# A spectral mixer and a long convolution, two layers each: the first loads, TensorE's first matmuls and five constant loads are put in another order

## The chip, the cores and the metric

One core of a Trainium2 chip runs the whole kernel. The metric is the device time of one execution in microseconds (us). The kernel before takes 1191.76 us in the median of three runs (1188.8 to 1192.48). Beside these runs there is one execution taken by the hardware profiler; every row quoted below comes from it.

## The reference

The input has 2048 positions of 576 channels. Four residual steps follow each other: spectral mixing, gated long convolution, and both once more.

```python
def _A_ref(x, dft_seq_re, dft_seq_im, dft_hid_re, dft_hid_im):
    a = jnp.einsum("bsd,ed->bse", x, dft_hid_re)
    b = jnp.einsum("bsd,ed->bse", x, dft_hid_im)
    y = jnp.einsum("ts,bse->bte", dft_seq_re, a) - jnp.einsum("ts,bse->bte", dft_seq_im, b)
    return y
...
x = x + _A_ref(_layernorm(x, axis=-1), ...)
x = x + _B_ref(_layernorm(x, axis=-1), ...)
x = x + _A_ref(_layernorm(x, axis=-1), ...)
x = x + _B_ref(_layernorm(x, axis=-1), ...)
```

`_B_ref` is a causal convolution of k with four taps, a product with v, a causal convolution over all 2048 positions by FFT of length 4096 with a kernel `ssm_k` of its own for each channel, a skip term and a product with q, which is the normed x. The result of the long convolution depends on k, v and the kernels alone, not on x. Both layers of B use the same k, v and kernels, so it is computed once.

## The kernel before, in words

**Numbers in two parts.** All large products run in the fp32r type with each operand split in two: the high part is a rounded copy (ScalarE, `split`, L98), the low part the rest (VectorE, `split`, L99). A product takes three matmuls: high by high, high by low, low by high.

**Layer 1, sequence product** (`layer`). The output positions are cut into four blocks `tb` of 512, the transform into cosine and sine `g`, the summed positions into 16 groups `k` of 128. One step `n` is one triple (tb, g, k). It multiplies group `k` of the normed x with a 128x512 tile of the matrix C: 12 matmuls into four PSUM banks `s0` to `s3` and two into `rm` for the last 64 channels, 14 in all. Within steps 0 to 15 every group of x is needed for the first time; later steps find all of x in SBUF. After 16 steps the banks are read out to `u` (`evac_u`, `evac_r`), and the hidden product (`hidden`, PSUM name `bk`) follows.

**How a group of x is made.** `load_x` (L680) issues its load of 288 KB on SyncE's queue. For groups 0 to 7 VectorE takes the statistics (`norm_stats`, L181 to L183: two `bn_stats`, `bn_aggr`, an addition), GpSimd raises them to the power -0.5 (L184), VectorE makes the bias (L190), ScalarE scales the row (L191). From group 8 on (`ASTAT = 8`) ScalarE takes the sums (`sums`, L649 and L651) with one small VectorE operation behind each (L650, L652), GpSimd the power (L653), VectorE the bias (L675), ScalarE the scaled row (L676). For all groups ScalarE then rounds the row (L195), and VectorE makes the two low parts (L197 of 64 columns, L198 of 512). `get_x0` (L691) calls these, one group ahead with `stats0`. `layer` asks for groups up to three ahead (`XLEAD = 3`).

**How a tile of C is made.** `load_c` (L210) loads 256 KB on SyncE's queue into the ring `craw` (three buffers at this time) and splits it into the ring `cs`, which has three buffers: the high part of tile n+3 can be written only when step n has read its own.

**The other work of the same stretch** (`branch`, a generator). Its first stage transforms `ssm_k` and v: a row of `ssm_k` or v (288 KB, SyncE's queue, L418) is split into `f1r`, multiplied with a constant `f1c[j]` (128 KB) by groups of six matmuls (PSUM names `bf0` to `bf2`, `f1_products`), read out by ScalarE (L451) and stored by ScalarE's queue (L452). I call such six matmuls a bf group. The convolution of k runs on VectorE in pieces of 128x1152 (`convolve`, L393 and L398), with the product with v at L426. The constant of the first j is loaded on SyncE's queue and rounded by ScalarE (L415, L416); those of the others on GpSimd's queue by `load_fr` (L170), which puts the load behind the newest power operation on GpSimd that was traced so far.

**What sets the order.** A scheduler of the framework orders the instructions of each engine. The source ties some of it down: `behind(i, ...)` (and `tc.issue_after(i)`) put what is traced inside behind `i` on the engine of `i`. The driving loop at L772 advances `branch` until `used` reaches `want`, a count that grows with the step n. Ahead of that loop stands the start (L746 to L768): it loads x group 0, the first `ssm_k` row and the first constant, makes group 0, splits the rows of `ssm_k` for the first two bf groups, and loads C tiles 0 and 1 and x groups 1 and 2 in between.

```python
want = int(4 + F1_16 * at / 8 if at <= 16 else at16 + (68 - at16) * (at - 16) / (F1_END - 16))
with behind(made[min(n + 2, J - 1)], *evac):
    while used < want:
        next(br)
        used += 1
```

After the first layer's sequence product come the middle and last stages of the long convolution, mixed with the hidden products, then layer 2 with a Strassen form of the same product and its hidden products.

Of the kernel before, what the change touches and what calls it, by code (L numbers as in the profile page):

```python
# [10 lines left out]
F32 = mybir.dt.float32  # L11
FR = mybir.dt.float32r
AF = mybir.ActivationFunctionType
# [17 lines left out]
K_FIRST = 4  # L31
F1_16 = 5
VW = 384
F1_END = 42
W_FROM = 41
HOLD = 125
# [29 lines left out]
def fnet_h3_kernel(ctx: ExitStack, tc: tile.TileContext, x, c_mat, w_re, w_im, k_pad, v, shift_k,  # L66
# [7 lines left out]
    def mm(ps, lhsT, rhs, first, last, more=False):  # L74
        return nc.tensor.matmul(ps, lhsT, rhs, start=first, stop=last, skip_group_check=more).ins  # L75
# [3 lines left out]
    def turn():  # L79
        given[0] += 1  # L80
        return banks[(given[0] - 1) % 3]
# [19 lines left out]
    @contextmanager  # L101
    def behind(*instructions):
        with ExitStack() as stack:
            for i in instructions:
                stack.enter_context(tc.issue_after(i))
            yield
# [54 lines left out]

    anchor, made, rounded, pows, biased, halved, added, evac, parted, stored = [], [], [], [], [], [], [], [], [], []

    scaled = []

    def load_after(dst, src):
        with tc.issue_after(anchor[-1]):
            return nc.sync.dma_start(dst, src).ins

    def load_fr(dst, src):  # L170
        with tc.issue_after(pows[-1]):
            nc.gpsimd.dma_start(dst, src)

    nc.vector.memset(mhalf, -0.5)
# [2 lines left out]
    def norm_stats(src):  # L177
        m = ring["stat"]()
        st, mv, ve, rs = m[:, :12].rearrange("p (a c) -> p a c", a=2), m[:, 12:14], m[:, 14:15], m[:, 15:16]
        for i in range(2):  # L180
            nc.vector.bn_stats(st[:, i, :], src[:, i * HD:(i + 1) * HD])  # L181
        nc.vector.bn_aggr(mv, st)
        nc.vector.tensor_scalar(ve, mv[:, 1:2], EPS, None, op0=OP.add)  # L183
        pows.append(nc.gpsimd.tensor_tensor(rs, ve, mhalf, OP.pow).ins)  # L184
        return mv, rs, m[:, 16:17]

# [23 lines left out]
    X = [None] * J  # L210
    CT = {}

    def load_c(step):
        g, tb, k = step
        raw = ring["craw"]()
        anchor.append(load_after(raw, c_mat[g, tb, k]) if anchor else nc.sync.dma_start(raw, c_mat[g, tb, k]).ins)
        c = ring["cs"]()
        t = c[:, :NT], c[:, NT:]
        with behind(*stored):
            halved[:] = split(t[0], t[1], raw)  # L220
        CT[step] = t

# [126 lines left out]
    def branch():  # L349
# [55 lines left out]
        def f1_loads(upto):  # L405
            while loads[0] < min(upto, len(todo)):
                j, src = todo[loads[0]]
                loads[0] += 1
                if j not in fcs:
                    fcs[j] = two(ring["fc"]())  # L410
                    if pows:
                        load_fr(fcs[j], f1c[j])
                    else:
                        raw = two(tmp[:, :2 * P])
                        nc.sync.dma_start(raw, f1c[j])  # L415
                        nc.scalar.activation(fcs[j], raw, AF.Copy)  # L416
                landed[j, src] = ring["land"]()
                nc.sync.dma_start(landed[j, src], (ssm_k if src else v)[:, j, :])  # L418
                if src and j == 0:
                    nc.sync.dma_start(tmp[:1, D:], ssm_d[None, :])  # L420
# [73 lines left out]
        at = lay(flts, SC_AT + CRAW * NT, ("res", D, 2))  # L494
        lay(flts, at, ("land", D, 2), ("kk", D, 2), ("vo", HD, 4))
        mc = quads(ring["mc"]())
        load_fr(mc, midc)
        lo, hi = slice(0, 64), slice(64, 128)

        def mid_half(df, o):  # L500
# [80 lines left out]
        def load_fc(k):  # L581
            if k < len(rows):
                fcs[k] = two(ring["fc"]())
                load_fr(fcs[k], i2c[rows[k]])

        def split_feed(i):
            if i < len(feeds):
# [87 lines left out]
        nc.vector.tensor_tensor(nb, sm, rs, OP.mult)  # L675
        nc.scalar.activation(y, src, AF.Identity, bias=nb, scale=rs)  # L676

    XL, LN = {}, {}

    def load_x(j):  # L680
        if j < J:
            XL[j] = ring["x"]()
            nc.sync.dma_start(XL[j], x[:, j, :])

    def stats0(j):
        if j < J and j not in LN:
# [4 lines left out]
    def get_x0(j):  # L691
        if X[j] is None:
            if j > 0:
                load_x(j + 2)
            stats0(j)
            if j > 0:
                with behind(*stored):
                    stats0(j + 1)
            src, ln = LN[j]
            with behind(*rounded[-1:]):  # L700
                next(ln, 0)
            X[j] = to_x(src, j)
# [32 lines left out]
    def done1(j, xa):  # L735
# [7 lines left out]
        if j < J - 1:  # L743
            nc.sync.dma_start(out[:, j, :], q)

    pending = []  # L746
    lay(flts, SC_AT, ("craw", NT, CRAW))
    br = branch()
    wl = load_w()
    load_x(0)  # L750
    next(br)
    get_x0(0)
    with tc.issue_after(biased[0]):
        next(br)
        with behind(*parted, scaled[0]):
            load_c((0, 0, 0))
        load_x(1)
        with behind(rounded[0]):
            load_c((0, 0, 1))
        load_x(2)  # L760
    used = 4
    first_lo = parted[1]
    next(br)
    next(br)
    with behind(first_lo):
        get_x0(1)
    next(br)
    next(br)  # L768
    spent = passed = 0.0
    total = (I2_END + 1 - MID_FROM) * STEP + 3 * 2 * TB * PIECE  # L770
    work = 64 * 3.1 + 32 * I2_COST
    for n, whole in layer(get_x0, lambda j: x[:, j, :], done0, pending):  # L772
        part = whole == "part"
        if part:
            whole = False
        if (whole or whole is not None and n % J < J - 1) and n <= F1_END and not part:
            at = n if whole else n - 0.5
            at16 = 4 + 2 * F1_16
            want = int(4 + F1_16 * at / 8 if at <= 16 else at16 + (68 - at16) * (at - 16) / (F1_END - 16))
            with behind(made[min(n + 2, J - 1)], *evac):  # L780
                while used < want:
                    next(br)
                    used += 1
        if whole is not None and not part and n >= W_FROM and len(W) < 9:
            with behind(*stored):
                next(wl)
        if whole and n == MID_LOAD:
            next(br)
        if n >= MID_FROM:
            if whole is not None:  # L790
                share = (5 if whole else 3) if n % J < J - 1 else (8 if whole else 6)
                passed += STEP * share / 14 * BORDER.get(n % J, 1.05)
            if whole is None or whole and n % 2 == 1 and n % (2 * J) < J - 1 and pending:
                finish(pending, 1)
                passed += PIECE
            while spent < work * min(1.0, passed / total):
                with behind(*added, *evac):
                    spent += next(br, work)
        if not whole:
            continue  # L800
        if n >= W_SAVE and n % 2 == 0:
            next(wl, 0)
# [352 lines left out]
```

## Time and profile before

| | |
|---|---|
| median of three runs | 1191.76 us (1188.8 to 1192.48) |
| profiled execution, its own time | 1191.32 us |
| its span, first to last instruction | 1189.5 us |
| TensorE matmuls busy | 1168.5 us, 98% of the span, 6184 matmuls |
| VectorE / ScalarE / GpSimd busy | 872.8 / 650.0 / 75.1 us |
| HBM traffic | 214 GB/s over the span; 326 GB/s in the first 56.52 us |

A row of the timeline has the start, the busy time, the engine (PE is TensorE, PEld its weight loads, DVE VectorE, ACT ScalarE, POOL GpSimd, SPq, ACTq and POOLq the issue of a transfer), the line, the operation, what it writes and reads, and how many equal ones are merged. In square brackets stands how long the engine had been idle before and what ended it. Neighbours on one engine overlap a little, so the distance between two starts is what an operation costs in a full queue. A row of the waits has the waiter, what it waited for, the sum in us, how often, and the longest. A row of the windows has for each engine its busy time and number of instructions, then the granted TensorE clock, the busy share of the DMA engines and the traffic.

### The profile page before, as it was taken

The page shows a single profiled execution, that of the slowest core. Times are in us where ns is not written, and L with a number is a line of the kernel's source. Part 1 is how long each engine was busy: PE and PEld are TensorE (multiplying, and loading weights), DVE is VectorE, ACT ScalarE, POOL GpSimd, SP SyncE. Part 2 cuts the span into 40 slices and gives each one's busy share as a digit, 9 for nine tenths or more (in the row PEclk, how much of TensorE's full clock was granted, in tenths as well). Part 3 has the DMA queues.
Part 4 walks back from the last instruction along what each step waited for, and adds up shares of the span by engine and source line. Part 5 has one row for each costly group of instructions (what it writes and reads, how often), then busy time and mean ns, then how long its engine had stood idle before and what let it go on. Part 6 is the DMA issues. An engine that isn't in the chain of part 4 may idle for free.

```text
span 1189.5 us, 18071 instructions
## 1 busy us (share of the span) xinstructions
PE 1168.5 (98%) x6184; PEld 987.2 (83%) x6184; DVE 872.8 (73%) x1562; ACT 650.0 (55%) x1279; POOL 75.1 (6%) x116
## 2 busy tenths in 40 slices
PE   7999999999999999999999999999999999999997
PEld 5776767888888888888888898888888888889997
DVE  7899983688777778787767665865776776775764
ACT  7865555567766668766645666534444445450200
POOL 2210000000000000001101111000000000001111
PEclk9999999999999999999999999999999999999999
DMA  9869898545656656648966777772772776795621
GB/s 340 295 197 306 269 290 267 178 139 177 225 189 198 200 160 204 186 137 239 273 197 226 235 246 231 251 250 73 255 248 71 240 273 248 266 322 158 214 83 41
DMA packets 147454, 255.65 MB, mean 215 GB/s; under 512 B 16161, under 2 KB 56353, under 8 KB 147362
## 3 DMA queue, kind: packets, MB, share of 16 engines
q1 hardware_dynamic: 111890, 210.17, 54.9%
q10 hardware_dynamic: 28560, 37.91, 9.1%
q0 software_dynamic: 6912, 6.43, 2.4%
q8 instruction: 48, 0.79, 0.3%
q14 instruction: 44, 0.36, 0.1%
HBM read 187.80 MB, written 66.65 MB: 214 GB/s over the span
## 4 chain that ended last, share of the span: by engine, by line
PE 76%; ACT 2%; DVE 2%; DMA 2%; issue 1%; POOLq 0%; ACTq 0%; DVEq 0%
PE s L75 42%; PE bk L75 29%; PE rm L75 4%; ACT flts L512 1%; ACT mid L512 1%; DMA t<-ud 1%; DVE mid L518 0%; DMA yb<-flts 0%; DMA flts<-vd 0%; DMA flts<-in_c_mat 0%; DVE flts L532 0%; DVE flts L530 0%; ACT u L98 0%; DVE flts L531 0%; DVE flts L533 0%
## 5 line engine op out<-in xcount | busy, mean ns | idle before, releaser
L75 PE MATMUL s<-mats 128*128 128x512 f32 x2088 | 543.0, 395 | 1.6 <-ACT mats L195 0.8
L75 PEld LDWEIGHTS s<-mats 128*128 128x128 f32 x2088 | 381.0, 188 | 83.2 <-issue 10.6
L99 DVE TENSOR_TENSOR mats<-flts,mats 128x512 fp32r<-128x512 f32 x206 | 141.0, 688 | 50.8 <-ACT mats L98 48.4
L98 ACT ACTIVATE mats<-flts 128x512 fp32r<-128x512 f32 x206 | 128.3, 628 | 82.6 <-PE bk L75 31.2
L75 PE MATMUL bk<-mid 128*128 128x288 f32 x704 | 127.7, 302 | 1.6 <-DVE flts L287 0.8
L75 PEld LDWEIGHTS bk<-mid 128*128 128x128 f32 x704 | 108.0, 188 | 23.7 <-ACT flts L512 5.8
L512 ACT ACTIVATE flts<-bk 128x288 f32<-128x288 f32 (+1 forms) x192 | 76.3, 406 | 90.8 <-PE bk L75 75.9
L75 PE MATMUL bk<-w,u 128*128 128x288 f32 x864 | 121.3, 296 | 1.0 <-DVE w L241 0.4
L75 PEld LDWEIGHTS bk<-w,u 128*128 128x128 f32 x864 | 117.3, 188 | 5.5 <-DVE flts L532 1.7
L518 DVE TENSOR_TENSOR mid<-flts,mid 128x576 fp32r<-128x576 f32 (+1 forms) x149 | 93.4, 629 | 18.6 <-ACT mid L512 15.2
L75 PE MATMUL rm<-mats 128*128 128x512 f32 x304 | 94.6, 391 | 0.2 <-ACT flts L512 0.2
L512 ACT ACTIVATE mid<-flts 128x576 fp32r<-128x576 f32 (+1 forms) x148 | 80.3, 575 | 11.8 <-DVE flts L533 8.5
L287 DVE TENSOR_TENSOR flts<-flts,bk 128x288 f32<-128x288 f32 x48 | 21.8, 453 | 65.8 <-PE bk L75 65.7
L451 ACT ACTIVATE flts<-bf 128x384 f32<-128x384 f32 (+1 forms) x104 | 43.2, 463 | 46.0 <-PE bf L75 45.9
L75 PE MATMUL bk<-mats 128*128 128x288 f32 (+1 forms) x376 | 67.8, 317 | 0.0
L75 PEld LDWEIGHTS rm<-mats 128*128 128x128 f32 x304 | 56.9, 188 | 12.8 <-ACT flts L512 0.6
L75 PE MATMUL s<-t,mats 128*128 128x512 f32 x264 | 65.4, 390 | 0.6 <-DVE t L99 0.3
L184 POOL TENSOR_TENSOR flts<-flts 128x1 f32<-128x1 f32 x35 | 28.7, 821 | 522.4 <-DVE flts L183 522.3
L75 PE MATMUL bk<-mats,t 128*128 128x288 f32 (+1 forms) x368 | 59.3, 303 | 0.0
L512 ACT ACTIVATE flts<-flts 64x288 f32<-64x288 f32 x128 | 56.6, 443 | 4.7
L75 PEld LDWEIGHTS s<-t,mats 128*128 128x128 f32 x264 | 49.4, 188 | 11.7 <-DVE t L99 0.8
L75 PEld LDWEIGHTS bk<-mats 128*128 128x128 f32 x376 | 55.5, 188 | 3.4
(146 smaller groups left out, 1496.7 us busy)
## 6 DMA issues: line engine op xcount, KB each, us to landing
flts<-in_c_mat SPq DMA_DIRECT2D x148, 256.0 KB, 3.3
ph<-in_c_mat SPq DMA_DIRECT2D x54, 512.0 KB, 4.5
flts<-in_c_mat SPq DMA_DIRECT2D x30, 512.0 KB, 4.8
flts<-td SPq DMA_DIRECT2D x53, 288.0 KB, 2.9
td<-flts ACTq DMA_DIRECT2D x36, 384.0 KB, 4.6
vd<-flts ACTq DMA_DIRECT2D x64, 144.0 KB, 2.7
flts<-vd SPq DMA_DIRECT2D x32, 288.0 KB, 4.1
ud<-ph ACTq DMA_DIRECT2D x12, 512.0 KB, 6.3
```

The costliest lines, as they stand in the source:

```text
L75: return nc.tensor.matmul(ps, lhsT, rhs, start=first, stop=last, skip_group_check=more).ins
L98: a = nc.scalar.activation(h, src, AF.Copy).ins
L99: return a, nc.vector.tensor_tensor(l, src, h.bitcast(F32), OP.subtract).ins
L184: pows.append(nc.gpsimd.tensor_tensor(rs, ve, mhalf, OP.pow).ins)
L287: added[:] = [nc.vector.tensor_tensor(r[:, cs], r[:, cs], ps[:, :HD], OP.add).ins]
L451: stored[:] = [nc.scalar.activation(so[:, i, :], ps[i], AF.Copy).ins]
L512: last_act.append(nc.scalar.activation(*args, **kw).ins)
L518: nc.vector.tensor_tensor(l, src, h.bitcast(F32), OP.subtract)
```

## The change

The start is rewritten. SyncE's queue first gets x group 0, C tile 0, x group 1, C tile 1, x group 2, and no row of `ssm_k` among them. VectorE writes zeros into a 128x512 stretch of x group 15, and TensorE runs 18 matmuls of 128x512 on it into a `bf` bank (`warm`). C tile 0 is split ahead of x group 0's rounding, and its low part stands behind the variance of group 1 on VectorE. The first branch work stands behind the newest x load; `used` starts at -1, and `want` is held down to 2n-2 in the first steps, so no bf group comes before step 3 (two came before and inside step 0). The branch work of steps 0 to 7 is also put behind the newest x and C loads. The first five `f1c` loads go on GpSimd's queue, each behind one of the first five power operations in turn; the path by SyncE and ScalarE (L415, L416) is not taken any more. `get_x0` puts the next x load behind the newest C load and, for the first groups, the next group's statistics behind the low part of the group before.

In the two built programs VectorE's instructions stand in the same order again from the end of step 15 on, but for one pair, ScalarE's soon after that, and TensorE's from step 20 on. The `bf` banks are taken in another rotation.

```diff
+WARM = 18
...
-    def load_fr(dst, src):
-        with tc.issue_after(pows[-1]):
+    def load_fr(dst, src, *order):
+        with behind(*order):
             nc.gpsimd.dma_start(dst, src)
...
-        nc.vector.tensor_scalar(ve, mv[:, 1:2], EPS, None, op0=OP.add)
+        varied.append(nc.vector.tensor_scalar(ve, mv[:, 1:2], EPS, None, op0=OP.add).ins)
...
-    def load_c(step):
+    def raw_step(step):
         g, tb, k = step
         raw = ring["craw"]()
         anchor.append(load_after(raw, c_mat[g, tb, k]) if anchor else nc.sync.dma_start(raw, c_mat[g, tb, k]).ins)
+        return raw
+
+    def load_c(step, raw=None):
+        raw = raw_step(step) if raw is None else raw
         c = ring["cs"]()
         t = c[:, :NT], c[:, NT:]
-        with behind(*stored):
+        with behind(*stored, *rounded[step[2] - 2:max(0, step[2] - 1) if step[:2] == (0, 0) else 0]):
             halved[:] = split(t[0], t[1], raw)
...
-                        load_fr(fcs[j], f1c[j])
+                        load_fr(fcs[j], f1c[j], pows[-1 if len(fcs) > 5 else min(len(fcs), len(pows)) - 1])
...
             if j > 0:
-                load_x(j + 2)
+                with behind(anchor[-1]):
+                    load_x(j + 2)
             stats0(j)
             if j > 0:
-                with behind(*stored):
+                with behind(*stored, *made[j - 1:j if j < ASTAT - 1 else 0]):
                     stats0(j + 1)
...
+    def warm():
+        t = xs[:, J - 1, :NT]
+        nc.vector.memset(t.bitcast(F32), 0.0)
+        b = turn()
+        for i in range(WARM):
+            mm(b, t[:, :P], t, i == 0, i == WARM - 1)
+
...
     load_x(0)
-    next(br)
-    get_x0(0)
-    with tc.issue_after(biased[0]):
-        next(br)
-        with behind(*parted, scaled[0]):
-            load_c((0, 0, 0))
-        load_x(1)
-        with behind(rounded[0]):
-            load_c((0, 0, 1))
-        load_x(2)
-    used = 4
-    first_lo = parted[1]
-    next(br)
-    next(br)
-    with behind(first_lo):
-        get_x0(1)
-    next(br)
-    next(br)
+    raws = []
+    for i in range(2):
+        with behind(loaded[-1]):
+            raws.append(raw_step((0, 0, i)))
+        with behind(anchor[-1]):
+            load_x(i + 1)
+    warm()
+    stats0(0)
+    first = ring["cs"]()
+    CT[0, 0, 0] = first[:, :NT], first[:, NT:]
+    nc.scalar.activation(first[:, :NT], raws[0], AF.Copy)
+    next(LN[0][1], 0)
+    with behind(biased[0]):
+        stats0(1)
+    with behind(loaded[-1]):
+        next(br)
+    with behind(varied[1]):
+        low = nc.vector.tensor_tensor(first[:, NT:], raws[0], first[:, :NT].bitcast(F32), OP.subtract).ins
+        X[0] = to_x(LN[0][0], 0)
+    with behind(made[0]):
+        next(LN[1][1], 0)
+    with behind(biased[1], rounded[0]):
+        load_c((0, 0, 1), raws[1])
+    with behind(halved[1]):
+        stats0(2)
+    used = -1
...
-            want = int(4 + F1_16 * at / 8 if at <= 16 else at16 + (68 - at16) * (at - 16) / (F1_END - 16))
-            with behind(made[min(n + 2, J - 1)], *evac):
+            want = int(min(2 * at - 2, 4 + F1_16 * at / 8) if at <= 16 else at16 + (68 - at16) * (at - 16) / (F1_END - 16))
+            with behind(made[min(n + 2, J - 1)], *evac, *rounded[min(n, 4) + 1:min(n, 4) + 2],
+                        *(loaded[-1:] + anchor[-1:] if n < 8 else [])):
```

More of the change, by code (lines that the diff above doesn't have):

```diff
@@ L162, in fnet_h3_kernel @@
     anchor, made, rounded, pows, biased, halved, added, evac, parted, stored = [], [], [], [], [], [], [], [], [], []
-    scaled = []
+    scaled, varied = [], []
     def load_after(dst, src):
@@ L496, in branch @@
         mc = quads(ring["mc"]())
-        load_fr(mc, midc)
+        load_fr(mc, midc, pows[-1])
         lo, hi = slice(0, 64), slice(64, 128)
@@ L583, in load_fc @@
                 fcs[k] = two(ring["fc"]())
-                load_fr(fcs[k], i2c[rows[k]])
+                load_fr(fcs[k], i2c[rows[k]], pows[-1])
         def split_feed(i):
@@ L676, in normed_x @@
         nc.scalar.activation(y, src, AF.Identity, bias=nb, scale=rs)
-    XL, LN = {}, {}
+    XL, LN, loaded = {}, {}, []
     def load_x(j):
@@ L682, in load_x @@
             XL[j] = ring["x"]()
-            nc.sync.dma_start(XL[j], x[:, j, :])
+            loaded.append(nc.sync.dma_start(XL[j], x[:, j, :]).ins)
     def stats0(j):
```

## Prediction

> **What bounds the kernel now.** I read the page first. Matmuls fill 98% of the span, so a gain has to come from the small rest, and from matmuls that run slowly.
>
> ```profile
> PE 1168.5 (98%) x6184; PEld 987.2 (83%) x6184; DVE 872.8 (73%) x1562; ACT 650.0 (55%) x1279; POOL 75.1 (6%) x116
> ```
>
> TensorE's waits over the whole span come next, then its timeline at the start.
>
> ```profile
> PE bf L75 <- DVE f1r L99: 6.6, 1, 6.6
> PE bf L75 <- ACT flts L451: 1.7, 3, 1.2
> PE s L75 <- ACT mats L195: 0.8, 1, 0.8
> ```
>
> ```profile
> 6.58 1.09 PE L75 MATMUL bf<-f1r 64*128 64x288 f32 x6 [6.58 <-DVE f1r L99]
> 7.82 0.79 PE L75 MATMUL s<-mats 128*128 128x512 f32 x1
> ...
> 10.95 4.46 PE L75 MATMUL s<-mats 128*128 128x512 f32 x10
> 15.26 0.63 PE L75 MATMUL rm<-mats 128*128 128x512 f32 x2
> 15.73 2.90 PE L75 MATMUL s<-mats 128*128 128x512 f32 x12
> 18.47 0.61 PE L75 MATMUL rm<-mats 128*128 128x512 f32 x2
> ...
> 22.19 0.67 PE L75 MATMUL bf<-f1r 64*128 64x288 f32 x6
> 22.78 3.05 PE L75 MATMUL s<-mats 128*128 128x512 f32 x12
> ...
> 56.52 1.91 PE L75 MATMUL s<-mats 128*128 128x512 f32 x6 [0.77 <-ACT mats L195]
> ```
>
> The first wait ends at 6.58 us, and then matmuls run at half pace: ten of 128x512 take 15.26 - 10.95 = 4.31 us, 0.431 each; twelve from 15.73 on take 2.74, 0.228 each. A step of 14 costs 3.17, a bf group 22.78 - 22.19 = 0.59. At 15.73 TensorE has done step 0 and two bf groups, worth 3.17 + 2 x 0.59 = 4.35 at full pace, as if it had begun at full pace at 11.38.
>
> Whether anything else could follow a faster TensorE is seen in windows cut at points of VectorE's work: first statistics at 3.64, low parts of group 7 done at 30.48, low parts of group 12 begun at 56.82. The columns are PE, PEld, DVE, ACT, POOL.
>
> ```profile
> 3.64:15.73 12.09, 8.47 (x27) 5.85 (x28) 10.45 (x33) 8.78 (x17) 4.35 (x7) 1.00 1.03 362
> 15.73:30.48 14.75, 14.75 (x71) 11.55 (x70) 11.83 (x38) 13.52 (x26) 3.06 (x5) 1.00 1.04 369
> 30.48:56.82 26.34, 25.57 (x123) 19.59 (x122) 22.48 (x46) 22.54 (x51) 7.26 (x6) 1.00 0.90 310
> 56.82:104.60 47.78, 46.32 (x230) 33.80 (x229) 46.08 (x63) 27.84 (x58) 4.76 (x7) 1.00 0.72 219
> ```
>
> In the last window VectorE idles 1.70 us of 47.78. TensorE is tied to it: a split of `f1r` ends and the bf group that reads it starts within about 1 us.
>
> ```profile
> 101.86 0.76 DVE L99 TENSOR_TENSOR f1r<-flts,f1r 128x576 fp32r<-128x576 f32 x1
> ```
>
> ```profile
> 103.58 0.79 PE L75 MATMUL bf<-f1r 64*128 64x384 f32 x6
> ```
>
> So a TensorE that comes to this stretch early waits there for VectorE, unless VectorE comes early too. **What VectorE gains by 56.8 us is what the kernel can keep.** Before that, from 3.64 on, it idles 1.64 + 2.92 + 3.86 = 8.42 us. Its waits, 3.6 to 30.5 and then 30.48 to 56.9:
>
> ```profile
> DVE flts L190 <- POOL flts L184: 1.0, 2, 0.7
> DVE mats L99 <- ACT mats L98: 0.7, 2, 0.5
> DVE flts L652 <- ACT early L651: 0.7, 1, 0.7
> DVE flts L675 <- POOL flts L653: 0.7, 1, 0.7
> DVE mats L197 <- ACT mats L195: 0.5, 1, 0.5
> DVE flts L650 <- ACT early L649: 0.4, 1, 0.4
> ```
>
> ```profile
> DVE flts L675 <- POOL flts L653: 3.0, 5, 0.7
> DVE flts L652 <- ACT early L651: 0.8, 2, 0.5
> ```
>
> That is 4.7 us for powers on GpSimd and 3.1 for ScalarE; the rest of the 8.42 is small gaps and one late load.
>
> **The change part by part.**
>
> *TensorE's start.* The first step needs x group 0 rounded. Its statistics start when the load lands, and the load is first in the queue in both kernels.
>
> ```profile
> 3.64 0.82 DVE L181 BATCH_NORM_STATS2 flts<-early 128x6 f32<-128x288 f32 x2 [2.77 <-DMA early<-in_x]
> ```
>
> ```profile
> 5.81 0.87 ACT L191 ACTIVATE early<-early,flts 128x576 f32<-128x576 f32 x1
> 6.58 0.61 ACT L98 ACTIVATE mats<-flts 128x512 fp32r<-128x512 f32 x1
> 7.10 0.67 ACT L195 ACTIVATE mats<-early 128x576 fp32r<-128x576 f32 x1
> ```
>
> Before, a split of C (6.58) stands between scaling and rounding. Without it rounding starts at 5.81 + 0.87 = 6.68, and the first matmul 0.72 later (7.10 to 7.82): 7.4. Ahead of it go the 18 zero matmuls. VectorE's zeros have no row: above the 0.06 of a 128x1 memset, below the 0.69 of a two-input operation of that width; I take 0.69, from 0.87 to 1.56. It hides in the wait for x. If all 18 ran at half pace they would end at 1.56 + 18 x 0.431 = 9.3. The stretch from 10.95 was slow for at most 4.8 us; after as much, 11 are done at 6.4, and 7 x 0.228 more end at 8.0. So step 0 starts at full pace between 7.4 and 9.3; I take 8.0, 3.4 us ahead of the 11.38 above. The half-pace matmuls are gone, and what is late next is VectorE.
>
> By the Trainium skill (TensorE: Matmul & The Clock Gate, section on the HAM clock gate) the array doubles its clock after about 3.4 us of sustained work. With that the 18 would end at 7.2 and the head start would be 4.0 instead of 3.4; the slow stretch of up to 4.8 us above, behind single matmuls from 7.82 on, neither proves nor excludes it.
>
> *Loads.* C tile 3 now stands behind x 0 to 5, C 0 to 2, one `ssm_k` row and about two `f1c`: with itself 6 x 0.295 + 4 x 0.262 + 0.295 + 2 x 0.131 = 3.37 MB. The traffic of the first 30 us in 40 slices sums to 3.48 MB at 12.0.
>
> ```profile
> GB/s 0 0 92 344 361 275 297 372 335 299 317 359 397 395 395 399 403 375 376 404 402 400 379 376 384 415 355 378 388 353 324 361 354 399 406 399 353 283 356 354
> ```
>
> So tile 3 lands about 12. In the new order ScalarE's scaling of group 2 stands behind its split, so step 2 cannot start before 12.0 + 0.61 + 0.87 + 0.72 = 14.2; with step 0 at 8.0 it is due at 8.0 + 2 x 3.17 = 14.3. A landing half a us later would be paid in full by TensorE; I take 0. The five `f1c` loads hold GpSimd 0.69 each, between powers that are over 2 us apart: nothing, or, where a power follows at once, at most that.
>
> ```profile
> 4.97 0.55 POOL L184 TENSOR_TENSOR flts<-flts 128x1 f32<-128x1 f32 x1 [4.53 <-DVE flts L183]
> 5.48 0.69 POOL L172 DMA_DIRECT2D f1r<-in_f1c  x1
> ```
>
> *VectorE to the low parts of group 12.* The two instruction orders give the same operations up to there, but for one low part of C fewer in the new one (0.60 us). So its gain is 8.42 + 0.60 less the new idle time. That follows from where each bias stands. Directly behind the operation that feeds its power: groups 0, 3, 7, 8, 10, 13 and 14, at 0.66: 4.6 us. With a run of two-input operations in between: groups 1, 5, 9, 11, 12. What that does, one place of before shows:
>
> ```profile
> 49.25 2.62 DVE L393 TENSOR_TENSOR f1f<-f1f 128x1152 f32<-128x1152 f32 x2
> 51.79 0.76 DVE L99 TENSOR_TENSOR f1r<-f1f,f1r 128x576 fp32r<-128x576 f32 x1
> ...
> 53.59 0.16 DVE L675 TENSOR_TENSOR flts<-flts 128x1 f32<-128x1 f32 x1 [0.38 <-POOL flts L653]
> ```
>
> ```profile
> 49.42 4.13 POOL L653 TENSOR_TENSOR flts<-flts 128x1 f32<-128x1 f32 x1 [7.69 <-DVE flts L652]
> ```
>
> The power takes 4.13 instead of 0.55 and ends 0.4 after the run: 5 x 0.4 = 2.0. ScalarE's waits I bound by 0 and by the old 3.1 plus 1.1 twice (groups 8 and 10, where the square of a row stands behind another row's scaling): 5.3. I take 2.1, the old 3.1 without most of the early 0.7 and 0.5, which came behind the two `ssm_k` rows. Sum: 4.6 + 2.0 + 2.1 = 8.7, a gain of 9.02 - 8.7 = 0.3 us. From both sides: 4.6 alone gives a gain of 4.4, 4.6 + 2.0 + 5.3 = 11.9 a loss of 2.9.
>
> By the Trainium skill (SBUF — State Buffer, section on who interferes with whom) a VectorE instruction with two SBUF inputs and a GpSimd instruction that reads SBUF exclude each other for one whole instruction. The 4.13 agrees that they exclude each other, but it lasted over several instructions; rival 3 below is this case of one instruction.
>
> *From 57 us on* the orders agree but for neighbours. VectorE's 1.70 us of idle time there are left as they are. **Sum: 1191.32 of the profiled execution (1189.5 and 1.82 around it) - 0.3 = 1191.0.** The median of before is 0.44 above the profiled time, so this is 0.8 below the median.
>
> **The rivals.**
> 1. *The head start is kept.* VectorE's waits shrink to the powers that stand directly in its way. For it: in the window 15.73 to 30.48 TensorE is busy all the time while VectorE idles 2.92, so TensorE paced it. Against it: the windows after 30. Time: 3.4 to 4.0 less, capped by 4.4: 1187.6.
> 2. *Slower: a held power makes TensorE wait at step 11.* In the new order the power of group 11 starts in front of a 128x1152 piece, group 10's low parts, another piece and a low part of C, and group 11's own low parts then stand ahead of those of C tile 11 (0.73 by L197 and L198 of the distances 0.13 and 0.60). If that run has no gap, the power costs 4.13 - 0.55 = 3.6 more, as at 49.42, and all that follows is late. It decides only where TensorE already stands at step 11 for this group: 3.6 + 0.7 - 0.3: 1195.3 or a little more. Against it: at 49.42 the same event cost TensorE only the 0.77 at 56.52.
> 3. *A power waits for one instruction only, not for the run.* Once power and run did overlap in part:
>
> ```profile
> 36.42 1.35 DVE L393 TENSOR_TENSOR f1f<-f1f 128x1152 f32<-128x1152 f32 x1
> ```
>
> ```profile
> 35.98 0.93 POOL L653 TENSOR_TENSOR flts<-flts 128x1 f32<-128x1 f32 x1 [6.35 <-DVE flts L652]
> ```
>
> This power ended at 36.91, inside the piece that began at 36.42. If that is the usual case, the five powers end within their runs, the 2.0 goes, and the gain is 2.3: 1189.0. Against it stands the 4.13.
> 4. *The zeros do not bring TensorE to full pace.* Then step 0 runs from 9.3 to 9.3 + 14 x 0.431 = 15.3, as late as before, and there is no head start to give back. By VectorE's sum the end stays near 1191.5.
>
> **How the numbers follow.** Given back to VectorE: 0.46, at 1191.0, own range 1189 to 1193. One instruction only: 0.12. Head start kept: 0.27. Slower: 0.11. No full pace: 0.04. The bounds of VectorE's sum are 1191.3 - 4.4 = 1186.9 and 1191.3 + 2.9 = 1194.2; I take 1187.0 to 1194.2, which leaves the slower rival outside. A measurement of this kernel tells 0.3%, 3.6 us, from no change: faster is below 1188.2, slower above 1195.3. Faster 0.27, the kept case; slower 0.11; the other three, 0.62, within.
>
> **What would show it.** The first real matmul near 8 us and all steps at 3.17 show the start right. TensorE ahead by about 3 us up to step 8 (41.26 before), and idle at steps 8 to 12 for low parts of C or rows of x, show the giving back; step 12 then starts near 56. VectorE's idle time from 3.64 to the low parts of group 12 should be near 8.7. A step 12 near 53 would show rival 1 and my sum of VectorE's waits wrong; a GpSimd power of 4 us at group 11 with TensorE idle behind it, rival 2; powers of 0.55 to 0.95 in groups 5, 9, 11 and 12, rival 3; matmul distances of 0.43 after 9 us, rival 4.

## The result, and the profile after

The changed kernel takes 1192.83 us in the median of 13 runs (1191.5 to 1195.95), the kernel before 1190.86 in 13 runs beside it: ratio 1.0020, 95% interval 1.0011 to 1.0028. **It is about 2 us slower.** Forecast was 0.3 us faster than the profiled execution of before. The time lies inside the range of 1187.0 to 1194.2, the direction does not agree. The profiled execution took 1194.64 us, with a span of 1192.6.

In what follows the changed kernel's line numbers are 1 to 5 above those of before: L76 is the matmul, L99 and L100 are the two halves of a split, L185 and L658 the powers, L196 the rounding of x.

TensorE's timeline of the changed kernel, at the start and at steps 10 to 12:

```profile
1.49 5.96 PE L76 MATMUL bf<-mats 128*128 128x512 f32 x18 [1.49 <-DVE mats L754]
7.45 3.21 PE L76 MATMUL s<-mats 128*128 128x512 f32 x12
...
15.07 3.30 PE L76 MATMUL s<-mats 128*128 128x512 f32 x12 [0.76 <-ACT mats L196]
...
49.21 2.11 PE L76 MATMUL s<-mats 128*128 128x512 f32 x8 [0.63 <-DVE flts L655]
...
54.61 2.11 PE L76 MATMUL s<-mats 128*128 128x512 f32 x8 [0.71 <-DVE flts L655]
...
57.67 1.67 PE L76 MATMUL s<-mats 128*128 128x512 f32 x5 [0.71 <-ACT mats L196]
```

The start is as forecast: step 0 at 7.45 (8.0 forecast), at nearly full pace (its twelve 128x512 matmuls take 3.05 us, those of step 1 2.74). Step 2 is due at 14.3 and starts at 15.07. At steps 10 and 11 TensorE waits for low parts of C, which VectorE makes at 48.47 and 53.87 (the rows name L655, the small operation right behind them), and step 12, at 56.52 before, starts at 57.67. The whole lead is gone, and 1.15 us more.

Where step 2 was lost, by the timelines of SyncE, ScalarE and VectorE:

```profile
4.50 0.99 SPq L688 DMA_DIRECT2D early<-in_x  x2
7.78 0.33 SPq L169 DMA_DIRECT2D flts<-in_c_mat  x1
...
12.91 0.63 ACT L99 ACTIVATE mats<-flts 128x512 fp32r<-128x512 f32 x1 [2.67 <-DMA flts<-in_c_mat]
...
13.58 0.69 DVE L100 TENSOR_TENSOR mats<-flts,mats 128x512 fp32r<-128x512 f32 x1 [1.17 <-ACT mats L99]
```

C tile 3 is issued at 7.78, when the place of C tile 0 comes free, and lands at 12.9, not at 12.0 (in two more profiles of this kernel its split starts at 12.5 and 13.0). ScalarE stands still for 2.67 us, with the scaling of group 2 behind the split; VectorE waits 1.17, TensorE the 0.76 above.

VectorE's waits from 3.6 to 58, and its window from its first statistics to the low parts of group 12 (busy columns PE, PEld, DVE, ACT, POOL):

```profile
DVE flts L680 <- POOL flts L658: 3.5, 6, 0.7
DVE flts L191 <- POOL flts L185: 2.5, 4, 0.7
DVE flts L657 <- ACT early L656: 2.2, 3, 1.0
DVE flts L182 <- DMA early<-in_x: 2.2, 1, 2.2
DVE mats L100 <- ACT mats L99: 1.2, 1, 1.2
DVE mats L198 <- ACT mats L196: 0.2, 1, 0.2
```

```profile
3.64:57.97 54.33, 50.83 (x231) 36.90 (x231) 44.42 (x115) 43.99 (x88) 17.35 (x20) 1.00 0.94 323
97.00:100.00 3.00, 1.34 (x10) 0.66 (x8) 3.00 (x4) 1.96 (x4) 0.00 (x0) 1.00 0.80 265
100.00:104.00 4.00, 4.00 (x15) 2.61 (x14) 3.29 (x5) 2.08 (x5) 0.37 (x1) 0.57 0.89 274
```

VectorE idles 54.33 - 44.42 = 9.91 us (8.42 before, 8.7 forecast): 6.0 for powers, 3.6 for ScalarE. The two later windows show something new: after a wait at 97.6 TensorE's granted clock is 0.57 for 4 us.

A marker that later work cannot blur is VectorE's first split of `u`, when the sequence product of the first block ends. Before, then after:

```profile
70.59 2.48 DVE L99 TENSOR_TENSOR u<-s,u 128x512 fp32r<-128x512 f32 x4
```

```profile
72.33 2.47 DVE L100 TENSOR_TENSOR u<-s,u 128x512 fp32r<-128x512 f32 x4
```

The changed kernel is 1.74 us behind there, and 1.15 at group 12. The other 0.60 is the low part of C that the prediction counted as one fewer: it was only put off, and is paid between the two points.

### The profile page after: what moved, and what is told of

The parts are those of the page before. It is cut to its first block, busy times and chain, and to the rows that moved or that the text cites. A ratio compares the mean times of both kernels' runs of the same rounds, so it can differ in the third digit from the quotient of the medians.

```text
span 1192.6 us, 18112 instructions
## 1 busy us (share of the span) xinstructions
PE 1174.6 (98%) x6202; PEld 989.4 (83%) x6202; DVE 873.6 (73%) x1563; ACT 649.3 (54%) x1278; POOL 76.7 (6%) x117
## 4 chain that ended last, share of the span: by engine, by line
PE 73%; ACT 3%; DVE 3%; DMA 1%; issue 1%; ACTq 0%; POOLq 0%; DVEq 0%; SPq 0%
PE s L76 41%; PE bk L76 28%; PE rm L76 4%; ACT flts L517 1%; DVE mid L523 1%; ACT mid L517 1%; DMA flts<-in_c_mat 1%; DVE flts L537 0%; DVE flts L536 0%; DMA flts<-vd 0%; DVE flts L535 0%; ACT mats L99 0%; DMA yb<-flts 0%; ACT u L99 0%; DVE u L100 0%
## 5 line engine op out<-in xcount | busy, mean ns | idle before, releaser
L76 PE MATMUL s<-mats 128*128 128x512 f32 x2088 | 543.3, 395 | 3.5 <-ACT mats L196 1.5
L76 PEld LDWEIGHTS s<-mats 128*128 128x128 f32 x2088 | 379.3, 188 | 87.0 <-issue 10.8
L100 DVE TENSOR_TENSOR mats<-flts,mats 128x512 fp32r<-128x512 f32 x205 | 140.2, 688 | 51.3 <-ACT mats L99 49.4
L99 ACT ACTIVATE mats<-flts 128x512 fp32r<-128x512 f32 x205 | 127.5, 627 | 82.7 <-PE bk L76 29.5
L76 PE MATMUL bk<-mid 128*128 128x288 f32 x704 | 127.7, 302 | 1.4 <-DVE flts L292 0.6
L76 PEld LDWEIGHTS bk<-mid 128*128 128x128 f32 x704 | 108.0, 188 | 23.6 <-ACT flts L517 5.5
L76 PE MATMUL bk<-w,u 128*128 128x288 f32 x864 | 121.5, 296 | 1.6 <-DVE flts L537 0.7
L76 PEld LDWEIGHTS bk<-w,u 128*128 128x128 f32 x864 | 117.1, 188 | 6.8 <-DVE flts L537 2.4
L76 PE MATMUL rm<-mats 128*128 128x512 f32 x304 | 95.1, 391 | 0.1
L292 DVE TENSOR_TENSOR flts<-flts,bk 128x288 f32<-128x288 f32 x48 | 21.8, 453 | 66.8 <-PE bk L76 66.7
L76 PE MATMUL bk<-mats 128*128 128x288 f32 (+1 forms) x376 | 67.8, 317 | 0.0
L76 PEld LDWEIGHTS rm<-mats 128*128 128x128 f32 x304 | 56.8, 188 | 12.7 <-DVE mats L198 0.6
L76 PE MATMUL s<-t,mats 128*128 128x512 f32 x264 | 65.0, 389 | 0.0
L185 POOL TENSOR_TENSOR flts<-flts 128x1 f32<-128x1 f32 x35 | 29.1, 831 | 522.4 <-DVE flts L184 519.4
L76 PE MATMUL bk<-mats,t 128*128 128x288 f32 (+1 forms) x368 | 59.3, 303 | 0.0
L76 PEld LDWEIGHTS bk<-mats 128*128 128x128 f32 x376 | 55.6, 188 | 3.4
L76 PEld LDWEIGHTS s<-t,mats 128*128 128x128 f32 x264 | 49.4, 188 | 10.6 <-DVE t L100 0.4
```

The source lines that it names most:

```text
L99: a = nc.scalar.activation(h, src, AF.Copy).ins
L100: return a, nc.vector.tensor_tensor(l, src, h.bitcast(F32), OP.subtract).ins
L292: added[:] = [nc.vector.tensor_tensor(r[:, cs], r[:, cs], ps[:, :HD], OP.add).ins]
```

## The experiments

Theory: VectorE sets the end of the first 100 us, and the late C tile 3 is what it lost. Rivals: TensorE's start is worth its length and another part loses more; or a wait on some other engine takes the lead back. "Marker" is the start of the first split of `u` on VectorE (70.59 before).

| kernel | us | before beside it | ratio, 95% interval | marker |
|---|---|---|---|---|
| changed, again | 1193.5 | 1190.78 | 1.0024 (1.0013 to 1.0034) | 71.89 |
| C tile 3 in its own place | 1190.68 | 1190.78 | 1.0001 (0.9992 to 1.0010) | 71.16 |
| before + zeros | 1189.72 | 1190.78 | 0.9990 (0.9982 to 0.9999) | 68.83 |
| changed, no zeros | 1195.14 | 1190.78 | 1.0042 (1.0030 to 1.0055) | 73.28 |
| before + zeros, order of before | 1191.15 | 1190.67 | 1.0008 (0.9999 to 1.0016) | 69.74 |
| before, order made for zeros | 1188.53 | 1190.67 | 0.9981 (0.9971 to 0.9990) | 68.68 |
| changed, no zeros, its order | 1196.05 | 1190.67 | 1.0046 (1.0033 to 1.0059) | 72.84 |
| own place, two waits filled | 1191.62 | 1190.67 | 1.0011 (1.0002 to 1.0020) | 72.72 |
| before, thinned | 1189.69 | 1190.5 | 0.9990 (0.9982 to 0.9999) | 68.93 |
| changed, thinned | 1189.18 | 1190.5 | 0.9993 (0.9984 to 1.0002) | 69.74 |
| changed, `f1c` late | 1198.67 | 1190.5 | 1.0069 (1.0056 to 1.0082) | 78.79 |
| own place, no zeros | 1194.3 | 1190.5 | 1.0037 (1.0023 to 1.0050) | 71.73 |

**The changed kernel once more.** No edit.

> The changed kernel once more, for a second profile and more times. Theory (VectorE sets the end of the first 104 us; it was 1.74 us late from 72 us on, and the rest of the profiled 3.1 us came from TensorE's clock falling behind a wait of 1.66 us at 97.6): 1.5 to 2.5 us above the kernel before, and low parts of group 12 near 58.0 in the profile again. If TensorE's clock falls to about 0.6 in 100 to 104 us again, the fall belongs to the wait; if the wait is there and the clock is 1.00, the fall is a matter of chance and no part of the cause.

Slower again, group 12 at 57.53. But TensorE waits only 0.61 us at 97.8, and its clock stays at 1.00. The fall in the first profile is thus not what makes the kernel slower.

**Zeros alone, on the kernel before.**

```diff
+    def warm(): (as in the change, 14 matmuls)
     load_x(0)
+    warm()
     next(br)
```

> The kernel before with 14 zero matmuls ahead of its first real one, and nothing else of the change. Theory (VectorE bounds the start): TensorE's matmuls run at full pace from about 8 us on, TensorE waits instead, step 12 starts at 56.5 as before, and the time is that of the kernel before within 0.5 us. Rival (TensorE's start is worth its length, and some other part of the change loses more): 2 to 3 us faster than before.

1.06 us faster: neither theory. But the scheduler had also made another order of it, so the run does not tell pace from order.

**The changed kernel without its zeros.**

```diff
-    warm()
     stats0(0)
```

> The changed kernel without its zeros and the 18 zero matmuls; all else as in the changed kernel. Theory: steps 0 and 1 run at half pace and end some 3 us later, TensorE's waits at steps 10 and 11 go in exchange, and the time is that of the changed kernel within 0.7 us, 1 to 2.5 us above the kernel before. Rival (TensorE's start is worth its length): 2 to 3 us slower than the changed kernel.

1.6 us slower than the changed kernel; here too the order had changed. So the next ones hold the order.

**C tile 3 in a place of its own.**

```diff
-        raw = ring["craw"]()
+        raw = early[:, 10 * D:10 * D + NT] if own else ring["craw"]()
...
+                if n == 0 and i == 1 and get_x is get_x0:
+                    with behind(loaded[-1]):
+                        early_raw.append(raw_step(steps[3], True))
```

> The changed kernel with C tile 3 loaded right behind x row 3 into a place of its own, instead of waiting until 7.78 us for the place of C tile 0. It should land near 9 to 10 us instead of 12.9. Theory: VectorE's 1.17 us and TensorE's 0.76 us of waiting for it go, VectorE's low parts of group 12 start near 56.8 instead of 57.97, and the time is 1 to 1.5 us below the changed kernel, up to 2.7 below it if the clock stays up at 100 us. Rival (the late tile cost TensorE alone, which waits for VectorE later anyway): no change against the changed kernel.

VectorE, ScalarE and TensorE keep their order up to 76 us. x 4, x 5 and the `ssm_k` row go one load later, and C tile 4 takes the place at 7.88. Its timelines of SyncE, ScalarE, VectorE and TensorE:

```profile
4.02 0.43 SPq L169 DMA_DIRECT2D early<-in_c_mat  x1
...
11.28 0.63 ACT L99 ACTIVATE mats<-early 128x512 fp32r<-128x512 f32 x1 [0.94 <-PE rm L76]
...
12.43 0.67 DVE L100 TENSOR_TENSOR mats<-early,mats 128x512 fp32r<-128x512 f32 x1
...
14.48 2.88 PE L76 MATMUL s<-mats 128*128 128x512 f32 x12
...
71.16 2.47 DVE L100 TENSOR_TENSOR u<-s,u 128x512 fp32r<-128x512 f32 x4
```

The split now waits for TensorE to free its place and not for the load; VectorE's 1.17 and TensorE's 0.76 are gone, step 2 starts at 14.48. Group 12 is at 56.80, as in the kernel before (56.82). Since the order up to there is that of the changed kernel, this microsecond belongs to the tile. The time is that of the kernel before as well, 2.8 us below the changed kernel, but that the tile alone is worth 2.8 us is not shown: the marker moves by 0.7 to 1.2 only, and from 76 us on the scheduler has made another order here too. The last two profiles of this section show a place where that order gains.

**Zeros, in the order of before.** Every engine's order is tied to that of the built kernel before, by edges that make nothing wait:

```diff
+    for was, now in zip(names, names[1:]):
+        tc.add_manual_dep(by[now], was, NoSync)
```

> The kernel before with 14 zero matmuls, as in the run with zeros alone, but with the order of the instructions on every engine tied to that of the kernel before (with the zeros alone, the scheduler had also put 30 instructions of VectorE elsewhere). Theory (TensorE's pace at the start reaches the end only through another order on VectorE): the time of the kernel before within 0.5 us, VectorE's low parts of group 12 near 56.8. Rival (a full-pace TensorE frees ScalarE's evacuations, and these VectorE, in any order): 1 to 2 us faster than before, group 12 near 55.

The same order with a full-pace TensorE gains 0.85 us at the marker and nothing at the end. That is the theory's time, but not its path: group 12 starts at 55.98, not near 56.8, and a lead of 1.0 us is still there at 250 us. Where it goes is shown behind the last of the kernels below.

**The order made for zeros, without them.**

> The complement: the kernel before without zeros, with the order that the scheduler made for it with zeros. Theory (the order is what counts): as fast as the run with zeros alone, about 1 us below the kernel before, group 12 near 54.5. Rival (the pace counts): the kernel before or up to 2 us slower, since this order was made for another pace.

Order alone: 0.9981, the fastest kernel of this study, 2.1 us below the kernel before; VectorE idles 50.48 - 43.59 = 6.89 us up to group 12 instead of 8.42:

```profile
3.83:54.31 50.48, 47.38 (x217) 35.87 (x218) 43.59 (x114) 43.95 (x88) 16.71 (x18) 1.00 0.98 351
```

**The changed kernel's order, without zeros.**

> The changed kernel without its zeros, with the changed kernel's own order of instructions kept on every engine. If the pace at the start is worth nothing to this order: within 0.5 us of the changed kernel, group 12 near 57.5 to 58. If it is worth something: 1 to 2.5 us slower than the changed kernel.

0.0022, or 2.6 us, slower than the changed kernel, though the marker shows only 0.4 to 1.0. Leaving out the zeros costs something in this order, against the theory; that it is the head start that is missed does not follow, as the last of the kernels below shows.

**Two waits filled.** On the kernel with C tile 3 in its own place: pieces of the convolution are put in front of the variances of groups 8 and 10.

> The changed kernel with C tile 3 in a place of its own, its order kept, and two 128x1152 pieces of VectorE's convolution moved ahead, into its waits of 0.94 and 0.97 us for the squares of groups 8 and 10 on ScalarE. Theory (VectorE bounds the first 100 us, and these two waits are what the new order lost beside C tile 3): VectorE is ahead by 1.3 to 1.9 us more at 65 us than with the place of its own alone, and the time is 1.0 to 1.7 us lower, below the kernel before. Rival (TensorE or the loads bound this stretch): no lower by over 0.5 us.

A miss. VectorE's timeline shows why for the first piece, and its neighbour for the second:

```profile
29.54 1.36 DVE L420 TENSOR_TENSOR f1f<-f1f 128x1152 f32<-128x1152 f32 x1 [1.41 <-DMA f1f<-in_k_pad]
...
45.49 0.16 DVE L679 TENSOR_SCALAR flts<-flts 128x1 f32<-128x1 f32 x1 [1.01 <-ACT early L678]
```

The first piece's row of k had not landed. The second filled the wait of group 10, and group 11's then grew to 1.01, since its square on ScalarE starts when group 10's scaling, now later, is done. So this does not tell what those waits are worth, only that they hang together. It tells something of the marker, too: this one stands 1.56 us behind that of the own place alone, and the ratio is only 0.0010, or 1.2 us, higher.

**Both kernels thinned.**

```diff
+                    w = slice(0, 64 if t and i < 4 else D)
-                        nc.vector.tensor_tensor(out_t[:, n], k, wt[3 - t][:, n], OP.mult)
+                        nc.vector.tensor_tensor(out_t[:, n, w], k[:, :, w], wt[3 - t][:, n, w], OP.mult)
```

> The kernel before, its order kept on every engine, with 24 of VectorE's 128x1152 convolution pieces (six of seven for each of the first four pairs of rows) computed on 64 of 576 columns: that part of the convolution is left out, and VectorE has about 1.1 us less to do 24 times, 27 us over the first 90. It is the base for the next kernel. TensorE should wait for VectorE no more between 40 and 105 us; the time should be 1 to 4 us below the kernel before.

> The changed kernel with the same pieces left out. Theory (the head start of the changed kernel is real, and only VectorE's work behind it takes it back): with that work gone it ends 2 to 3.4 us before the thinned kernel before. Rival (loads, ScalarE or the chain of powers take the head start back, whatever VectorE has to do): it ends within 1 us of the thinned kernel before, or later.

Both leave out part of the convolution. The rival's result: 1189.69 and 1189.18. Up to group 12 VectorE is busy 37.62 and 37.51 us, 7 less than the 44.76 and 44.42 of the full kernels, and TensorE's step 12 still starts at the same time in both. First the thinned kernel before, then the thinned changed one, with its ScalarE:

```profile
55.90 1.91 PE L92 MATMUL s<-mats 128*128 128x512 f32 x6 [0.77 <-ACT mats L212]
```

```profile
46.80 0.71 ACT L474 ACTIVATE flts<-bf 128x288 f32<-128x288 f32 x2 [1.71 <-PE bf L93]
47.40 0.63 ACT L116 ACTIVATE mats<-flts 128x512 fp32r<-128x512 f32 x1
47.92 0.78 ACT L674 ACTIVATE early<-early,flts 128x576 f32<-128x576 f32 x1
...
55.01 0.68 ACT L213 ACTIVATE mats<-early 128x576 fp32r<-128x576 f32 x1
...
55.74 1.90 PE L93 MATMUL s<-mats 128*128 128x512 f32 x6 [1.10 <-ACT mats L213]
```

Step 12 waits for x row 12 to be rounded (55.01). The row's square (47.92) had its input at 45.27, and stood on ScalarE behind an evacuation of TensorE's products (46.80), which itself waited 1.71 us for them, and a split of C; from 46.80 on ScalarE has no gap. With VectorE out of the way, what gives the lead back is, by these rows, the fixed order of ScalarE; no run has moved it.

**The `f1c` loads late.**

```diff
-    load_fr(fcs[j], f1c[j], pows[-1 if len(fcs) > 5 else min(len(fcs), len(pows)) - 1])
+    load_fr(fcs[j], f1c[j], pows[-1])
```

> The changed kernel with the first five loads of f1c each behind the last power issued, as in the kernel before; only GpSimd's order differs (8 lines). Theory (these loads cost nothing): the changed kernel within 0.5 us. Rival (they hold powers or take the DMA from C tile 3): 0.5 to 1.5 us faster than the changed kernel.

Against both: 0.0045, about 5.4 us, slower than the changed kernel. The second `f1c` load is issued at 24.53, behind the power of group 6 (8.14, behind group 1's, in the changed kernel), and TensorE waits for one of the late ones:

```profile
24.53 0.58 POOL L173 DMA_DIRECT2D f1r<-in_f1c  x1
...
32.70 1.09 PE L76 MATMUL bf<-f1r 64*128 64x288 f32 x6 [5.98 <-DMA f1r<-in_f1c]
```

C tile 3, issued at 7.99, is split at 12.84 here, with one `f1c` load issued before 12 us instead of three: the early `f1c` loads are not what made it late.

**Own place, no zeros, order kept.**

> The changed kernel with C tile 3 in a place of its own and without the zeros, order kept: what is left of the change is the order at the start alone. If order, C tile 3 and TensorE's pace add up on VectorE, it stands at 65 us some 0.5 to 0.9 us behind the same kernel with zeros, thus 1.1 to 1.5 us behind the kernel before, and ends 1 to 3 us above the kernel before. If C tile 3's place alone had been the fault of the new order, it ends with the kernel before.

Marker 1.14 behind the kernel before, 0.0037 slower. Order and pace do add up at the marker; leaving out the zeros costs more at the end (0.0036, about 4 us) than there (0.4 to 0.6).

**Where the zeros matter.** VectorE splits `u` again later on. The table has the start of such a split near 250 us and of one near 611 us, the same two in each kernel (the first profile of the changed kernel holds the lower clock at 100 us):

| kernel | marker | near 250 | near 611 | between these |
|---|---|---|---|---|
| before | 70.59 | 250.84 | 610.91 | 360.1 |
| before + zeros, order of before | 69.74 | 249.82 | 611.12 | 361.3 |
| changed, first profile | 72.33 | 254.35 | 614.73 | 360.4 |
| changed, again | 71.89 | 251.79 | 612.09 | 360.3 |
| changed, no zeros, its order | 72.84 | 252.48 | 615.99 | 363.5 |
| own place | 71.16 | 250.45 | 610.81 | 360.4 |
| own place, no zeros | 71.73 | 248.83 | 611.99 | 363.2 |

At 250 us no head start is missing: the own place without zeros is 1.6 us ahead of the one with them, and the changed kernel without zeros stands between two profiles with them. Without the zeros about 3 us are lost between 250 and 611 us, and in the order of before it is putting them in that loses 1.2 us there. (The profiled execution of the own place without zeros took 1191.77 us, below the median of 1194.3.) TensorE's waits from 300 to 350 us, first with zeros (changed), then without (changed, no zeros, its order):

```profile
PE bk L76 <- DVE flts L537: 0.3, 1, 0.3
```

```profile
PE bk L93 <- ACT flts L534: 0.7, 1, 0.7
PE bk L93 <- DVE flts L554: 0.2, 1, 0.2
```

These are waits for read-outs of `bk` banks in the middle stage of the long convolution, not for anything of the first 100 us. `warm` also takes one turn in the rotation of the three `bf` banks, so every later group has another bank with it than without it; whether that is the reason was not tested.

**Two more profiles,** one execution each.

> A third profile of the changed kernel. If the steps that its distance to the kernel before took at about 215 us (+0.5 in the second profile, 0.1 in the first) and 1035 us (+1.3 and 0) belong to the single execution, they come out otherwise again; VectorE's distance at 65 us should be 1.3 to 1.8 us once more, and TensorE's clock should stay up at 100 us unless it waits 1.6 us or more there.

> A second profile of the changed kernel with C tile 3 in a place of its own. If its distance to the kernel before is a matter of the load: 0.4 to 0.7 us at 65 us again, no fall of the clock at 100 us. If its steps at 215 us (-0.5) and 745 us (+1.1) belong to the kernel and not to the execution, they come again.

Markers 72.44 and 71.31, times 1194.35 and 1190.87. The clock stayed up in both. TensorE's waits from 200 to 225 us, first in the second profile of the changed kernel, then in that of the own place:

```profile
PE bk L76 <- DVE flts L292: 0.8, 1, 0.8
PE bk L76 <- ACT w L245: 0.6, 1, 0.6
PE bk L76 <- DVE w L246: 0.4, 1, 0.4
```

```profile
PE bk L76 <- ACT w L247: 0.5, 1, 0.5
PE bk L76 <- DVE w L248: 0.4, 1, 0.4
```

The wait of 0.6 to 0.8 for L292 is in all three profiles of the changed kernel and in neither of the own place. Lateness does not bring it: the kernel before has it (first row below, L287), and the kernel with two waits filled, as late as the changed kernel at the marker, has not. The order differs. In the changed kernel VectorE's read-out of a bank (L292) stands behind a split of C that waits for its load; with the own place the scheduler has put a split of C further ahead, and the read-out (there L294) waits for TensorE alone. The rows are of the kernel before, the changed kernel and the own place:

```profile
PE bk L75 <- DVE flts L287: 0.8, 1, 0.8
```

```profile
218.98 0.69 DVE L100 TENSOR_TENSOR mats<-flts,mats 128x512 fp32r<-128x512 f32 x1 [1.05 <-ACT mats L99]
219.70 0.46 DVE L292 TENSOR_TENSOR flts<-flts,bk 128x288 f32<-128x288 f32 x1
```

```profile
215.81 0.46 DVE L294 TENSOR_TENSOR flts<-flts,bk 128x288 f32<-128x288 f32 x1 [0.41 <-PE bk L76]
```

Between the matmuls that the kernel before starts at 207 and 219 us, the changed kernel loses 0.1 to 0.5 us on it, and the own place gains 0.5 in both profiles. So of the 2.8 us between these two kernels 0.6 to 1.0 arise near 210 us, where their orders differ. Steps at 745 and 1035 us came out differently in profiles of the same kernel.

## Why the prediction was wrong

**The step that failed is the loads:** "A landing half a us later would be paid in full by TensorE; I take 0." C tile 3 landed 0.9 later (0.5 to 1.0 in three profiles). With the tile in its own place, and the order the same up to there, group 12 comes 0.6 to 1.3 us earlier (56.80 and 56.94 against 57.53 to 58.08): that is the size of the term that was taken as 0. The ratio goes from 1.0024 to 1.0001 with it, but part of that is the other order near 210 us. The landing came from a sum of the bytes ahead of the tile. The same trace offered a better row, the median time from issue to landing in this stretch; here from the changed kernel's first 20 us, with its traffic in slices of 0.5 us:

```profile
GB/s 0 0 0 46 194 384 372 327 342 299 376 408 363 367 327 341 336 369 380 370 355 389 368 377 397 379 413 392 402 406 407 389 354 377 385 369 372 176 174 162
...
flts<-in_c_mat SPq DMA_DIRECT2D x7, 256.0 KB, 4.8
```

Up to 12.0 the traffic sums to 3.55 MB, more than the 3.37 counted, and the tile was not there. Which other bytes went ahead, or what fixed time a load needs beside its bytes, was not tested. Issue at 7.78 and 4.8 make 12.6. The issue time follows from the ring of three places, which the prediction did not follow to its end.

**VectorE's sum.** Powers: 6.6 taken, 6.0 measured. Idle time for ScalarE: 2.1 taken, 3.6 measured, of which the tile is 1.2. The low part of C, counted as a gain of 0.60, was only put off; without it the sum would have been a loss of 0.3 even with the tile in time. With the measured terms VectorE loses 9.91 - 8.42 = 1.49 in idle time, gains 0.60 up to group 12, and its operations take 0.26 longer (44.42 + 0.60 against the 44.76 of before): the 1.15 seen there, and 1.74 when the 0.60 is paid.

**"What VectorE gains by 56.8 us is what the kernel can keep"** was too strong. That the lead is given back by step 12 held, with a kernel that idles 9.91 us on VectorE where 8.7 was forecast. But the thinned pair points to ScalarE's order as the next bound, close behind: freeing VectorE of 7 us moves step 12 by 1.9 us in the changed kernel (57.67 to 55.74) and by 0.6 in the kernel before (56.52 to 55.90).

**TensorE's start** was right: 7.45 within 7.4 to 9.3 (7.54 and 8.43 in the other profiles of this kernel), zeros written in 0.48 us (0.69 taken). The 18 zero matmuls took 7.45 - 1.49 = 5.96 us, so about 9 went at 0.431 and the rest at 0.228; in the two profiles of the own place step 0 starts at 8.14 and 8.42, and about 13 and 14 went slowly. That is 4 to 6 us of work before full pace. By the Trainium skill (TensorE: Matmul & The Clock Gate, section on the HAM clock gate) it takes about 3.4 us, varying with the phase of a window that runs free; that agrees with the first profile, less well with the other two.

**The `f1c` loads** did not delay the tile, and no cost of theirs shows, as said; but the sum did not name what their earliness covers: 5.4 us, had the new order come without it.

**The rivals.** Head start kept: wrong for the changed kernel, where it is gone at step 12. In the order of before 1.0 us of it is kept up to 250 us and lost behind it (1.0008). The 2.6 us that leaving out the zeros costs the new order do not show a head start that was kept: in the profiles the loss without them falls behind 250 us. Step 11: group 11's power took 1.66 us, not 4, and TensorE waited 0.71 there, not 3.6. One instruction only: it was both; the held powers of groups 9, 11 and 12, in POOL's timeline, lasted about one piece, one piece, and a run:

```profile
38.69 1.59 POOL L658 TENSOR_TENSOR flts<-flts 128x1 f32<-128x1 f32 x1 [7.55 <-DVE flts L657]
...
45.29 1.66 POOL L658 TENSOR_TENSOR flts<-flts 128x1 f32<-128x1 f32 x1 [2.34 <-DVE flts L657]
51.36 3.60 POOL L658 TENSOR_TENSOR flts<-flts 128x1 f32<-128x1 f32 x1 [4.42 <-DVE flts L657]
```

Zeros without effect: no, full pace came.

**Open:** why the zeros change the stretch from 250 to 611 us, by 3 us one way in the new order and by 1.2 the other way in that of before; how much of the own place's 2.8 us the tile alone is worth at the end, beyond the microsecond at group 12; and the steps after 700 us.

## What to carry over

When a first load moves, follow its buffer to the instruction that frees it, and date its landing by issue plus the measured time to landing of its like, not by the bytes ahead of it; here a tile 0.9 us late held up the row scaled behind it on ScalarE, and with it TensorE by 0.76 and VectorE by 1.17 us. A lead on the busiest engine is worth only what the latency chains across the others leave of it, so look for the next bound behind the one you found. And an edit that a scheduler sees changes the order everywhere: tie the order down before reading a small difference as the effect of the edit (here the order alone was worth 2.1 us), and follow the difference along the whole span, because a part of it may arise hundreds of microseconds behind the edit.

## What the runs showed of the hardware

TensorE's clock can halve after a wait far shorter than the time it takes to come up (1.66 us in one case, against the 4 to 6 us of work above). In the changed kernel's first profile TensorE waited 1.66 us and then ran at 0.57 in the mean from 100 to 104 us. In the kernel with the order made for zeros it waited 1.72 us, and the clock was 0.50 behind it:

```profile
211.80 0.40 PE L92 MATMUL bk<-w,u 128*128 128x288 f32 x1 [1.72 <-ACT w L257]
```

```profile
213.60:217.00 3.40, 3.40 (x13) 2.92 (x12) 1.75 (x3) 0.65 (x2) 0.00 (x0) 0.50 0.59 175
```

The same followed waits of 2.27 us (changed, no zeros, at 53.9) and 5.98 us (`f1c` late, 32.7). After 2.28 us in the run of the new order without zeros (1044.4) the clock stayed at 1.00, and in all 16 profiles no wait of 1.23 us or less, the longest otherwise, brought a fall. By the Trainium skill (TensorE: Matmul & The Clock Gate, section on the HAM clock gate) a window of about 3.4 us that runs free decides; that would fit a clock that falls behind 2.27 us in one execution and not behind 2.28 in another, but not that 1.66 us are enough, where the page asks for an idle window.
